# The first attention batch in a new order, held-back transposes and loads, and weight sums placed earlier

## The chip, the cores and the metric

The kernel runs on one core of a Trainium2 chip. The metric is the device time of one execution in microseconds (us). Nine executions of the kernel before took 974.5 to 976.42 us, with a median of 975.21. The engines are called as in the profile: PE is TensorE (PEld its weight load), DVE is VectorE, ACT is ScalarE, POOL is GpSimd, SP is SyncE. POOL and SP issue nearly all DMA transfers.

## The reference

Two parts follow each other. The first is a linear attention with cosine weights over 8 batches, 8 heads, 576 positions and a head width of 64; the second a mixture of 8 experts over the 4608 rows that come out, with gate weights that are balanced by eight rounds of Sinkhorn scaling.

```python
theta = np.pi / 2.0 * pos / S
phi(x) = concatenate([relu(x) * cos(theta), relu(x) * sin(theta)])   # q_p, k_p
kv  = einsum('bhsf,bhfd->...', k_p, v);  z = sum(k_p over s)
num = q_p @ kv;  den = q_p @ z + 1e-06;  x = num / den               # per batch and head
P = exp(x @ w_gate - max)
for _ in range(8): P /= P.sum(1) + 1e-09; P /= P.sum(0) + 1e-09; P *= N / E
out = sum over e of P[:, e] * (relu(x @ w1[e]) @ w2[e])
```

## The kernel before

**Attention and expert 0 are interleaved.** Batch 0 is computed alone. Then come blocks of 512 rows of expert 0, index j from 0. Each block has 16 slots: in slots 0 to 7 `ffn1` makes one eighth of the hidden layer (four products of 512 columns and a relu on ACT), in slots 8 to 15 `ffn2` makes half a tile of 128 output rows (four products; every second slot ends with a copy of the tile on ACT). A table, filled by `at(block, slot, ...)` in lines 641 to 788, hangs the attention work of batch j + 1 and the preparation of batch j + 2 behind the slots. Slots 0 to 3 of block 0 are done with batch 0's numerators (lines 677 to 695). The instructions of PE, DVE and ACT stand in the order in which the code writes them (`InOrder`, line 101). Those of POOL and SP are placed by the framework, which keeps their dependencies.

**Steps of one batch**, with the names of the profile. `load` (line 229) brings q, k and v in halves of two head pairs, six transfers a batch, issued by POOL; `held_back` lets a load wait for the latest DVE instruction written so far. Each of the names q_ld, k_ld and v_ld has four buffers. `prep_q` (line 377) makes q_p, the scaled q of one head pair, on DVE. For batches 0 and 1 PE turns it against an identity matrix (`turn`, line 420), and ACT or DVE copies the result out of a `small_ps` bank (there are four) with a relu. From batch 2 on SP turns it with a DMA transpose into q_pT (line 392). `prep_k` is the relu on k (ACT or DVE), `prep_kp` makes k_p on DVE, `prep_v` copies v beside a column of constants. `sums` makes the products of k_p and v for half the heads and copies them to kv_sb; for batch 0 the key sums z come from PE products of their own (`key_sums`). `denominators` (line 527) makes the products with z for all heads, then DVE's reciprocal den, and hi and hl, two parts of it. `spread_out` repeats hl over rows on PE, ACT copies it to rb; `numerators` multiplies q_pT by kv_sb on PE, and DVE multiplies by rb into xT, the input of the experts.

One line of the transposes ties them to a load:

```python
                if b == 3 and hk == 0:

                    after(landing["v", b, 1], turned)
```

With b counted from 0 this is the fourth batch and its first head pair. `after` is a real wait, `not_before` only an order on one engine.

**Fillers.** `keep_busy` (line 276) gives PE products of ones with ones whose result nobody reads, at the start and wherever batch 0 leaves PE without work.

**Experts 1 to 7** use sums of weight blocks and of row blocks, so that fewer products are needed. `w1_steps` and `w1_sums` build such sums of w1, `w2_first` replaces a block of w2 by a difference, and `Pair.step` builds three more sums of w2 (tiles V, lines 1004 to 1017) when the first pair of an expert arrives. `group` (line 916) makes the hidden layer of one quarter of the columns for 768 rows; it calls `fill()` seven times. While the first unit of expert 1 runs, `start_fill` (line 1188) deals out the last tiles of expert 0 in parts and the remaining steps of `sinkhorn` (line 1071). In a Sinkhorn round, `tw_steps` (line 1143) lists the weight sums done meanwhile: the first two of a round behind its column sums, the others behind its product on PE. After that unit, `w2_first` for expert 1 runs on DVE (line 1248).

Of the kernel before, what the change touches and what calls it, by code (L numbers as in the profile page):

```python
# [19 lines left out]
XS = 64.0  # L20
# [5 lines left out]
def kernel(  # L26
# [185 lines left out]
    with ExitStack() as p1:  # L212
        ld = p1.enter_context(tc.tile_pool(name="ld", bufs=4))
        kp_pool = p1.enter_context(tc.tile_pool(name="kp_pool", bufs=4))
        qp_pool = p1.enter_context(tc.tile_pool(name="qp_pool", bufs=3))
        qT_pool = p1.enter_context(tc.tile_pool(name="qT_pool", bufs=1))
        kv_pool = p1.enter_context(tc.tile_pool(name="kv_pool", bufs=2))
        rb_pool = p1.enter_context(tc.tile_pool(name="rb_pool", bufs=4))
# [7 lines left out]
        landing = {}  # L226
        sources = {"q": q, "k": k, "v": v}

        def load(b, half, names="qkv", held_back=False):
            for name in names:  # L230
# [6 lines left out]
                if held_back:  # L237

                    after(ve.last, i)
# [8 lines left out]
        load(0, 0, "q")  # L248
        gidx = cs_pool.tile([P, C], FP32, name="gidx")
# [4 lines left out]

        ones_sq = cs_pool.tile([P, P], F16, name="ones_sq")
# [6 lines left out]
        load(0, 1, "q")  # L262
        for name in "kv":
            load(0, 0, name)
            load(0, 1, name)
# [22 lines left out]
        for _ in range(74):  # L288
            keep_busy(1)
# [17 lines left out]
        for hh in range(2):  # L307
            ve.tensor_copy(
                out=cs_half[hh * HP : (hh + 1) * HP, :, :, hh],
                in_=cs[hh * HP : (hh + 1) * HP, :, :, 0],  # L310
            )
# [8 lines left out]
        C3 = C // 3  # L320

# [6 lines left out]
        with nc.allow_low_precision("sums of zeros and ones"):  # L328
# [11 lines left out]
        ones_col = const.tile([P, 1], FP32, name="ones_col")  # L340
        ve.memset(ones_col[:], 1.0)
        ones_all = const.tile([P, P], FP32, name="ones_all")
        ve.memset(ones_all[:], 1.0)
        eps_row = cs_pool.tile([1, 32], FP32, name="eps_row")
        ve.memset(eps_row[:], 1e-6 / XS)
# [8 lines left out]
        lent = acc_lo[:, G_LO - 4 : G_LO, :].rearrange("p g d -> p (g d)").bitcast(F16)  # L354
        VA = C * (D + 2)
        v_augs = [
            lent[:, i * VA : (i + 1) * VA].rearrange("p (c d) -> p c d", d=D + 2)
            for i in range(4)
        ]
# [7 lines left out]
        for t in v_augs:  # L367
            ve.memset(t[:, :, D : D + 1], 1.0 / XS)

# [7 lines left out]
        def prep_q(b, hk):  # L377
# [12 lines left out]
            if by_dma:  # L390
                qTs[b, hk] = q_pTs[(b * HK + hk) % len(q_pTs)]
                turned = nc.sync.dma_start(
                    out=qTs[b, hk], in_=q_p[:].rearrange("p c a d -> p (c a d)"),
                    transpose=True,
                )
                if b == 3 and hk == 0:

                    after(landing["v", b, 1], turned)
            else:
                qps[b, hk] = q_p  # L400
# [76 lines left out]
        def sums_begun(b, half):  # L477
# [7 lines left out]
            kv_ps = [ps_s.tile([P, 512], FP32, name="small_ps") for hh in range(2)]  # L485
# [157 lines left out]
        for hk in range(HK):  # L643
            if hk == 3:
                prep_k(0, 0)
                prep_k(0, 1)
                z_ps = key_sums(0)
                prep_q(0, hk)
                key_sums_made(0, z_ps)
            else:  # L650
                prep_q(0, hk)
            for i in range(3):
                turn(0, hk, i, True)
                keep_busy(3)
        prep_kp(0, 0)
        prep_kp(0, 1)
        denominators(0, range(0, 4))
        keep_busy(8)
        for hk in (2, 3):
            prep_k(0, hk)  # L660
        z_ps = key_sums(1)
        prep_kp(0, 2)
        key_sums_made(1, z_ps)
        prep_kp(0, 3)
        keep_busy(5)
        denominators(0, range(4, 8))
        for half in range(2):
            sums_made(0, half, sums_begun(0, half))
            keep_busy((0, 18)[half])
# [6 lines left out]
        ]  # L676
        for hk in range(HK):
            attend(0, hk)
            for kt in ((), (0,), (1,), (2, 3))[hk]:
                for ft, h_ps in enumerate(first_ps):  # L680
                    te.matmul(
                        out=h_ps[:],
                        lhsT=w0[0][:, kt, ft * P : (ft + 1) * P],
                        rhs=xT[:, kt, 0:TCH],
                        start=(kt == 0),
                        stop=(kt == KT - 1),
                    )
                    if kt == KT - 1:
                        se.activation(out=hT[:, ft, 0:TCH], in_=h_ps[:], func=AF.Relu)
            for i in ((), (0,), (1, 2), ())[hk]:  # L690
                prep_k(1, i, i < 2)
            for i in ((), (0,), (1,), (2, 3))[hk]:
                if i == 3:
                    prep_k(1, i, False)
                prep_kp(1, i)
# [3 lines left out]
        for j in range(B):  # L699
            b = j + 1  # L700
            if j == 0:
# [4 lines left out]
                for hk in range(HK):  # L706
                    for i in range(3):
                        at(0, (5, 6, 6, 7)[hk], turn, 1, hk, i, i != 1)
                    if hk == 0:
                        at(0, 5, prep_q, 1, 3)  # L710
                    if hk == 2:
                        at(0, 6, prep_v, 1, 0, se.copy)
                        at(0, 6, prep_v, 1, 2, ve.tensor_copy)
                    if hk == 3:
                        at(0, 7, prep_v, 1, 1, se.copy)
                        at(0, 7, prep_v, 1, 3, ve.tensor_copy)
# [6 lines left out]
            elif b < B:  # L723
# [14 lines left out]
                elif j == 2:  # L738
                    at(j, 0, sums, b, 1)
# [554 lines left out]
```

## Time and profile before

| | us |
|---|---|
| median of nine executions | 975.21 |
| lowest, highest | 974.5, 976.42 |
| the profiled execution, time | 974.5 |
| its span, first to last instruction | 972.8 |

The page gives each engine's busy time within the span. A line of the timeline reads: start in us, duration in us, engine, line, operation, written tile <- read tiles, shapes, count, and in brackets how long the engine had been idle and what released it. Many lines say L109, the helper through which every PE, DVE and ACT instruction is issued; there the tiles' names tell the step. The chain that ended last is mostly PE:

```profile
PE 91%; DMA 4%; issue 2%; DVE 1%; POOL 1%; ACT 0%; POOLq 0%; DVEq 0%; SPq 0%; ACTq 0%
```

The granted clock is 1.00 in all parts. The DMA queues are busiest in the first 45 us, when the loads of three batches and the weights of expert 0 arrive.

### The profile page before, as it was taken

What the parts mean: (1) busy time and instruction counts of PE and PEld (TensorE: products, weight loads), DVE (VectorE), ACT (ScalarE), POOL (GpSimd) and SP (SyncE); (2) the same over time, 40 slices, a digit from 0 to 9 for tenths busy, and PEclk for the clock granted to TensorE, in tenths of its full rate; (3) what the DMA queues carried; (4) which work ended last, traced back from release to release, by engine and by line L of the source; (5) the groups of instructions that cost most, each with busy time, mean ns of one, the idle gap of its engine ahead of it and who ended that gap; (6) DMA issues with size and microseconds to landing.
All of it is one profiled execution on the core that took longest, in us unless ns stands there. A gap on an engine that the chain in (4) does not pass through costs nothing.

```text
span 972.8 us, 20258 instructions
## 1 busy us (share of the span) xinstructions
PE 960.5 (99%) x7855; PEld 675.9 (69%) x7855; DVE 807.3 (83%) x1831; ACT 565.5 (58%) x1264; POOL 60.7 (6%) x82
## 2 busy tenths in 40 slices
PE   9999999999999999999999999999999999999997
PEld 6545545567777777777777777777777777777775
DVE  6777776789898987987888987987888987988887
ACT  5766665577776555555555555555555555555551
POOL 6231110010000000000000000000000000000001
PEclk9999999999999999999999999999999999999999
DMA  9999988231004301332004301322104401104435
GB/s 163 184 152 178 153 141 185 44 69 50 26 26 93 69 25 50 68 59 59 25 26 93 69 25 51 68 51 64 30 25 85 77 25 42 33 27 126 122 90 127
DMA packets 81200, 74.72 MB, mean 77 GB/s; under 512 B 33360, under 2 KB 73040, under 8 KB 81104
## 3 DMA queue, kind: packets, MB, share of 16 engines
q0 software_dynamic: 27232, 30.94, 20.4%
q1 hardware_dynamic: 53632, 42.24, 17.4%
q8 instruction: 61, 1.00, 0.4%
q14 instruction: 35, 0.29, 0.1%
q10 hardware_dynamic: 240, 0.26, 0.1%
HBM read 84.30 MB, written 12.98 MB: 100 GB/s over the span
## 4 chain that ended last, share of the span: by engine, by line
PE 91%; DMA 4%; issue 2%; DVE 1%; POOL 1%; ACT 0%; POOLq 0%; DVEq 0%; SPq 0%; ACTq 0%
PE rows_ps L109 34%; PE h_ps L109 28%; PE p_ps L109 11%; PE copied_ps L109 11%; PE y_ps L109 4%; PE small_ps L109 3%; DMA k_ld<-in_k_dram 1%; DMA w2e<-in_moe_w_dram 1%; DMA w1e<-in_moe_w_dram 1%; DVE acc_hi L975 0%; POOL q_ld L233 0%; POOL hs_last L990 0%; DMA out_dram<-acc_lo 0%; DVE H L905 0%; DVE S L203 0%
## 5 line engine op out<-in xcount | busy, mean ns | idle before, releaser
L975 DVE SCALAR_TENSOR_TENSOR acc_lo<-rows_ps,P_tok,acc_lo 128x512 f32<-128x512 f32 (+1 forms) x322 | 203.2, 639 | 75.0 <-PE rows_ps L109 74.9
L109 PEld LDWEIGHTS <-H 128*128 128x128 f16 x2080 | 203.2, 98 | 82.3 <-issue 1.4
L911 ACT CAST u<-h_ps 128x384 f16<-128x384 f32 x288 | 137.7, 478 | 129.6 <-PE h_ps L109 129.6
L109 PEld LDWEIGHTS <-w1e 128*128 128x128 f16 x1632 | 157.7, 98 | 67.3 <-issue 5.3
L905 DVE CUSTOM_DVE_ANT_0 H<-p_ps,u 128x384 f16<-128x384 f32 x329 | 180.9, 550 | 7.3 <-PE p_ps L109 7.2
L109 PEld LDWEIGHTS <-hs 128*128 128x128 f16 x1500 | 146.6, 98 | 56.2
L109 PE MATMUL p_ps<-xT,T 128*128 128x384 f16 x672 | 164.1, 326 | 1.0 <-DVE H L905 0.9
L109 PE MATMUL h_ps<-S,w1e 128*128 128x384 f16 x672 | 164.1, 326 | 0.8 <-ACT u L911 0.6
L109 PE MATMUL rows_ps<-V,H 128*128 128x256 f16 x1000 | 150.0, 273 | 0.7 <-DVE acc_hi L975 0.7
L109 PE MATMUL rows_ps<-w2e,hs 128*128 128x256 f16 x1000 | 150.0, 273 | 0.0
L109 PE MATMUL h_ps<-xT,w1e 128*128 128x384 f16 (+1 forms) x616 | 148.8, 350 | 0.1
L943 ACT ACTIVATE H<-h_ps 128x384 f16<-128x384 f32 x144 | 70.7, 491 | 94.5 <-PE h_ps L109 94.5
L109 PEld LDWEIGHTS <-T 128*128 128x128 f16 x1008 | 98.4, 98 | 31.8 <-issue 4.8
L109 PE MATMUL rows_ps<-w2e,H 128*128 128x256 f16 (+1 forms) x568 | 94.4, 285 | 0.0
L924 ACT COPY copied_ps<-h_ps 128x384 f32<-128x384 f32 x144 | 67.4, 468 | 35.9 <-PE h_ps L109 35.1
L934 ACT ACTIVATE H<-copied_ps 128x384 f16<-128x384 f32 x144 | 70.9, 492 | 20.3 <-PE copied_ps L109 20.3
L109 PE MATMUL h_ps<-S,T 128*128 128x384 f16 x336 | 81.8, 325 | 0.6 <-ACT copied_ps L109 0.5
L109 PE MATMUL copied_ps<-xT,w1e 128*128 128x384 f16 x336 | 82.1, 326 | 0.0
L109 PE MATMUL copied_ps<-w2e,H 128*128 128x256 f16 x504 | 75.5, 272 | 0.0
L109 PE MATMUL rows_ps<-V,hs 128*128 128x256 f16 x500 | 75.0, 272 | 0.0
L975 DVE SCALAR_TENSOR_TENSOR acc_lo<-copied_ps,P_tok,acc_lo 128x256 f32<-128x256 f32 x126 | 60.0, 476 | 0.4
L975 DVE SCALAR_TENSOR_TENSOR acc_hi<-rows_ps,P_tok,acc_hi 128x512 f32<-128x512 f32 (+1 forms) x56 | 41.3, 737 | 20.6 <-PE rows_ps L109 19.8
(146 smaller groups left out, 948.2 us busy)
## 6 DMA issues: line engine op xcount, KB each, us to landing
S<-x_saved SPq DMA_DIRECT2D x114, 192.0 KB, 2.3
out_dram<-acc_lo SPq DMA_DIRECT2D x62, 128.0 KB, 2.4
w1e<-in_moe_w_dram POOLq DMA_DIRECT2D x7, 1024.0 KB, 9.1
w2e<-in_moe_w_dram POOLq DMA_DIRECT2D x7, 1024.0 KB, 10.0
q_ld<-in_q_dram POOLq DMA_DIRECT2D x16, 288.0 KB, 6.6
k_ld<-in_k_dram POOLq DMA_DIRECT2D x16, 288.0 KB, 8.3
v_ld<-in_v_dram POOLq DMA_DIRECT2D x16, 288.0 KB, 9.3
x_saved<-S SPq DMA_DIRECT2D x12, 192.0 KB, 1.8
```

Of the source, the lines that this page charges most:

```text
L109: i = getattr(self.engine, name)(*args, **kwargs)
L905: latest = ve._custom_dve(TENSOR_ADD_SAT, out=out, in0=ps[:, 0:TU], in1=t[:], s0=FP32_MAX, s1=0.0)
L911: se.copy(out=t[:], in_=ps[:, 0:TU])
L924: se.copy(out=Y[:, 0:TU], in_=X[:, 0:TU])
L934: se.activation(out=h11, in_=Y[:, 0:TU], func=AF.Relu)
L943: se.activation(out=h12, in_=X[:, 0:TU], func=AF.Relu)
L975: ve.scalar_tensor_tensor(out=a, in0=rows, scalar=P_tok[:, g, self.e : self.e + 1], in1=a, op0=ALU.mult, op1=ALU.add,)
```

## The change

The change has these parts.

- **Buffers.** q_p gets four buffers instead of three, rb three instead of four.
- **Setup.** The second half of q is issued ahead of the position index, the first half of k ahead of the identity mask. The 74 fillers of 128 columns become 110 of 64. Memsets move up, and the copy into `cs_half` moves behind the second q_p (`halve`).
- **Batch 0.** The four q_p come first, k after them; the second half of `sums` moves behind the second spread and uses the `h_ps` banks; the first products of expert 0 start with the two `y_ps` banks. k_p of batch 1 moves behind them all.
- **Block 0.** PE's turns of batch 1 move from slots 5, 6, 6, 7 to 6, 6, 7, 7, and all four v copies go to DVE.
- **Blocks 1 to 6.** Block 2 gets the schedule of the later ones; the relus of k stand three to five slots later; the first half of the sums of the fourth batch moves from block 1 to block 2, and so do part of its k_p and v.
- **Transposes and loads.** From the fourth batch on every transpose waits for the fifth of its batch's six loads, and the loads of a later batch (from index 4 on) wait for the second transpose of the batch before instead of for DVE.
- **Expert 1.** `w2_first` and the three V sums of expert 1 move into the Sinkhorn rounds; the parts of expert 0's last tiles are dealt out at other fills.

```diff
-        qp_pool = p1.enter_context(tc.tile_pool(name="qp_pool", bufs=3))
+        qp_pool = p1.enter_context(tc.tile_pool(name="qp_pool", bufs=4))
...
-        rb_pool = p1.enter_context(tc.tile_pool(name="rb_pool", bufs=4))
+        rb_pool = p1.enter_context(tc.tile_pool(name="rb_pool", bufs=3))
...
-                if held_back:
+                if behind is not None:
+
+                    after(turnings[behind], i)
+                elif held_back:
...
-        for _ in range(74):
-            keep_busy(1)
+        for _ in range(110):
+            te.matmul(
+                out=idle_ps[:, 0:HP], lhsT=ones_sq[:],
+                rhs=ones_sq[:, 0:1].to_broadcast([P, HP]), start=True, stop=True,
+            )
...
-                if b == 3 and hk == 0:
-
-                    after(landing["v", b, 1], turned)
+                if b >= 3:
+
+                    after(landing["v", b, 0] if b < 5 else landing["k", b, 1], turned)
+                turnings[b, hk] = turned
...
         for hk in range(HK):
+            prep_q(0, hk)
+            if hk == 1:
+                halve()
             if hk == 3:
                 prep_k(0, 0)
                 prep_k(0, 1)
                 z_ps = key_sums(0)
-                prep_q(0, hk)
-                key_sums_made(0, z_ps)
-            else:
-                prep_q(0, hk)
             for i in range(3):
                 turn(0, hk, i, True)
-                keep_busy(3)
+                keep_busy(3 * (hk < 3))
         prep_kp(0, 0)
+        key_sums_made(0, z_ps)
+        for hk in (2, 3):
+            prep_k(0, hk)
         prep_kp(0, 1)
         denominators(0, range(0, 4))
-        keep_busy(8)
-        for hk in (2, 3):
-            prep_k(0, hk)
         z_ps = key_sums(1)
+        keep_busy(4)
+        key_sums_made(1, z_ps)
         prep_kp(0, 2)
-        key_sums_made(1, z_ps)
+        denominators(0, range(4, 8))
         prep_kp(0, 3)
-        keep_busy(5)
-        denominators(0, range(4, 8))
-        for half in range(2):
-            sums_made(0, half, sums_begun(0, half))
-            keep_busy((0, 18)[half])
+        sums_made(0, 0, sums_begun(0, 0))
+        keep_busy(20)
+        spread_out(0, 0)
+        numerators(0, 0)
+        keep_busy(4)
+        spread_out(0, 1)
+        sums_made(0, 1, sums_begun(0, 1, (ps_h[0], "h_ps")))
...
+        numerators(0, 1)
+        spread_out(0, 2)
+        first_l1(0, (2, 3, 0, 1))
+        numerators(0, 2)
+        spread_out(0, 3)
+        first_l1(1, range(4))
+        numerators(0, 3)
+        prep_k(1, 0)
+        prep_k(1, 1)
+        first_l1(2, range(4))
+        first_l1(3, range(4))
         for hk in range(HK):
...
+            if hk >= 2:
+                prep_k(1, hk, False)
+            prep_kp(1, hk)
         for hk in range(3):
             prep_q(1, hk)
...
-                        at(0, (5, 6, 6, 7)[hk], turn, 1, hk, i, i != 1)
+                        at(0, (6, 6, 7, 7)[hk], turn, 1, hk, i, i != 1)
                     if hk == 0:
-                        at(0, 5, prep_q, 1, 3)
...
+                        at(0, 6, prep_q, 1, 3)
+                    if hk in (1, 3):
+                        for i in (hk - 1, hk):
+                            at(0, (6, 7)[hk // 2], prep_v, 1, i, ve.tensor_copy)
...
-                at(j, 6 if j == 1 else 3 if j == 2 else 4, denominators, b)
+                at(j, 6 if j == 1 else 4, denominators, b)
...
+                    (4, prep_q, 0), (5, prep_q, 1), (9, prep_k, 0), (8, prep_q, 2),
+                    (10, prep_k, 1), (12, prep_q, 3), (12, prep_k, 2), (13, prep_k, 3),
+                    (13, prep_kv, 0), (14, prep_kv, 1),
                 ) if j == 1 else (
...
+                    (5, prep_q, 0), (6, prep_q, 1), (8, prep_k, 0), (8, prep_q, 2),
+                    (9, prep_k, 1), (10, prep_q, 3), (10, prep_k, 2), (11, prep_k, 3),
                     (11, prep_kv, 0), (14, prep_kv, 1),
...
-                if j == 1:
-                    at(j, 15, sums, b + 1, 0)
...
-                        at(j, 12, load, b + 2, half, name, True)
+                        at(j, 12, load, b + 2, half, name, True, (b + 1, 1))
             elif j and b + 2 < B:
                 for half in range(2):
-                    at(j, 11 + half, load, b + 2, half, "qkv", True)
+                    at(j, 11 + half, load, b + 2, half, "qkv", True, (b + 1, 1))
...
+    nothing = [lambda: None] * 2
+    tw_steps[2].append(lambda: w2_first(w_next))
+    tw_steps[4].append(lambda: w2_sums(w_next[1], 0))
+    tw_steps[5] = nothing + [lambda: w2_sums(w_next[1], 1)]
+    tw_steps[6] = nothing + [lambda: w2_sums(w_next[1], 2)]
...
-        for _ in range(1 + (k_fill % 14 == 1)):
+        for _ in range(1 + (k_fill in (1, 2, 23))):
...
-                w2_first(w)
```

`first_l1(kt, fts)` is the loop of the kernel before over the four banks for one kt, with the relu behind the last. `w2_sums(w2, part)` holds the DVE sums that stood in `Pair.step`: two for part 0 and 1 (V of lines 1007 and 1008), one for part 2 (line 1017); experts from 2 on still call them where they stood. `sums_begun` takes the banks as an argument.

## The prediction

> **What bounds the kernel now.** I read the busy times of the page first, then busy time by stretches of 10 us, then the timeline where PE (TensorE) is not full.
>
> ```profile
> PE 960.5 (99%) x7855; PEld 675.9 (69%) x7855; DVE 807.3 (83%) x1831; ACT 565.5 (58%) x1264; POOL 60.7 (6%) x82
> ...
> 50.00:60.00 10.00, 8.95 (x115) 4.46 (x114) 7.41 (x17) 5.12 (x13) 3.59 (x5) 1.00 1.05 144
> 60.00:70.00 10.00, 9.68 (x119) 4.86 (x119) 8.18 (x19) 7.66 (x20) 2.96 (x5) 1.00 0.99 167
> 180.00:190.00 10.00, 9.54 (x51) 4.87 (x50) 7.88 (x21) 6.74 (x13) 0.75 (x1) 1.00 0.40 65
> 200.00:210.00 10.00, 9.01 (x61) 5.65 (x59) 9.90 (x21) 6.09 (x15) 3.36 (x3) 1.00 0.79 145
> ```
>
> The columns of the stretches: PE, PEld, DVE, ACT, POOL busy, granted clock, DMA share, GB/s. PE has no work to lose in this change except fillers, so only its waits and the fillers can move the time. From 70 to 180 us its busy time reads 10.00 in every stretch: edits there gain nothing and can only harm. What can be won lies in four places: the start (fillers hide its waits), 58 to 62, 189, and 203 to 207. DVE is nearly full in the last.
>
> The start, in the timeline:
>
> ```profile
> 10.87 0.53 DVE L109 TENSOR_SCALAR k_ld<-k_ld 128x576 f16<-128x576 f16 x2 [1.63 <-DMA k_ld<-in_k_dram]
> 11.31 0.75 DVE L109 TENSOR_TENSOR q_p<-q_ld,acc_hi 128x1152 f16<-128x1152 f16 x1
> 15.41 0.75 DVE L109 TENSOR_TENSOR k_p<-k_ld,acc_hi 128x1152 f16<-128x1152 f16 x1
> 16.11 1.35 DVE L109 RECIPROCAL den<-y_ps 96x192 f32<-96x192 f32 x1
> 17.79 0.42 DVE L109 SCALAR_TENSOR_TENSOR hl<-hi,lo,den 96x192 f16<-96x192 f16 x1
> 33.47 1.03 PE L109 MATMUL small_ps<-acc_lo,k_p 64*128 64x65 f16 x54 [0.74 <-ACT acc_lo L109]
> 34.44 1.04 PE L109 MATMUL y_ps<-w2e,hT 128*128 128x512 f16 x4
> ```
>
> DVE waits for the first keys, then works without a break from 10.87 to 18.21, when hl, on which every later product hangs, is done. The fourth q_p and the fourth k_p stand in this row ahead of hl. The row at 34.44 is slot 8 of block 0, my mark for the end of the start.
>
> Near 58 us:
>
> ```profile
> 54.19 3.20 SPq L392 DMA_TRANSPOSE q_pT<-q_p  x1
> 58.61 0.68 ACT L109 ACTIVATE k_ld<-k_ld 128x576 f16<-128x576 f16 x1 [2.39 <-DMA k_ld<-in_k_dram]
> 59.66 0.70 ACT L109 COPY rb<-small_ps 128x384 f32<-128x384 f32 x2
> 60.20 0.46 PE L109 MATMUL small_ps<-hl,acc_hi 96*128 96x192 f16 x3 [1.25 <-ACT rb L109]
> ```
>
> ACT stands in order: the relu of the fourth batch's first keys (slot 8) waits for their load, the rb copy that PE needs (slot 9) stands behind it. Expert 1:
>
> ```profile
> 189.00 0.58 ACT L109 COPY acc_hi<-rows_ps 128x512 f32<-128x512 f32 x1
> 190.02 0.48 PE L109 MATMUL h_ps<-S,T 128*128 128x384 f16 x2 [0.48 <-ACT copied_ps L109]
> ...
> 201.40 0.72 DVE L109 TENSOR_TENSOR w2e<-w2e 128x1024 f16<-128x1024 f16 x1
> 203.58 0.68 DVE L1007 TENSOR_TENSOR V<-w2e 128x1024 f16<-128x1024 f16 x1
> 204.51 0.68 DVE L1008 TENSOR_TENSOR V<-V,w2e 128x1024 f16<-128x1024 f16 x1
> 206.38 0.48 PE L109 MATMUL p_ps<-xT,T 128*128 128x384 f16 x2 [0.85 <-DVE H L905]
> ```
>
> Three weight sums sit in DVE's queue ahead of the add that frees PE's bank; and a 0.58 us accumulator copy sits ahead of the copy PE waits for.
>
> **1. First batch.** Queue order of the loads is unchanged except that iota and the mask stand one load later; POOL's loads are held by the landing of earlier ones up to batch 2 (each issue follows the landing of the eighth load before it: 10.84 to 11.13, 12.30 to 12.58), so no landing moves. The keys still come at 10.84. The 110 fillers of 64 columns: the 128-column ones ran 106.7 ns apart up to 6.97 us and 57.7 ns after. Per filler, from below half of 106.7, so an end near 7.0; from above 96 ns (7.09 us over 74) if the weight load held the pace, an end at 11.7 and about 3 us lost. The nearest row for a full weight load with few columns is the gate product, 20 in 0.66 us (33 ns, doubled at the slow start): 88 of them until 6.97, 22 more in 0.7, end 7.7. I take that; it lies beside the wait for keys.
>
> With four q_p buffers and the new order, the fourth q_p (0.75) is done before 10.84. DVE after the landing: two relus 0.44, k_p 0.67, zsel 0.25 after the key sums on PE (0.73) to 12.4, two relus and k_p 1.1 to 13.6, second zsel after its key sums to 14.1, k_p 0.67, reciprocal, hi, hl 1.39 + 0.29 + 0.42: about 16.9, and the fourth k_p behind it. That is 1.3 earlier than 18.21. PE then has four spreads (0.35), four numerators (0.36), 16 products (0.22), and now the second half of the sums and a filler (0.8), which lay ahead of hl before: 7.2 us, to 24.2 against 25.6.
>
> Then the work put last comes due: the four k_p, two relus and three q_p of batch 1 all stand behind the last xT product (23.2), 5.1 us of DVE, to 28.35; before, k_p ran between the xT products. PE's slots 4 to 6 (2.7) end at 26.9, its turns need q_p (27.1, 27.7) and then a bank that DVE empties only at 28.9: a new wait of 0.7. Slot 7, the fourth q_p, four evictions and four v copies (DVE now has all four, 0.44 each) bring the second sums to 33.1 against 34.4: **-1.2**. Ends: -2.2 (the second quarter of w2 lands at 32.14) and +0.5 (DVE's queue gives all back).
>
> **2. Fourth batch.** Its loads start at 51.67 and land 1.40, 1.90, 1.57, 1.83 apart, those of batch 2 about 1.4 apart; the transpose at 54.19 ran beside them and took 10.3 us to land. Held back, the keys come no later than now, and their relu moves behind the rb copy of slot 9. The PE idle time of 50 to 70 is 1.05 + 0.32: **-1.4**. If the keys are 1 us late again, ACT has the copy of slot 10 behind them: 0 is the other end.
>
> **3. The new wait.** Behind a waiting transpose on SP stand only transposes; behind a load that waits for the second transpose, on POOL, only loads. Who waits for both: the denominators of batch 4 (index 3), in block 2 slot 4. Block 2 began at 67.8; less 1.2, less 1.4 and less the 0.7 of half a sums group that moves from block 1 into it: 64.5. Slot 4's denominators come 5.8 to 6.3 later (block 3: 86.38 to 92.19), so the last transpose must have landed at about 70.6. The fifth load lands near 60.3 (start 50.4, first landing 5.5 later, three more at 1.45); transposes issue 1.4 apart: 60.3, 61.7, 63.0, 64.4. The second lands near 65.0 and releases the loads of batch 5, which meet the fourth. What does a transpose beside loads cost? Without loads beside it 3.2 to 3.7. The Trainium skill (DMA: Bandwidth & Descriptors, section Queues, rings and completion order) says that each engine takes turns between its queues packet by packet; by that rule a shared transpose takes at most twice its own time, 6.6, lands by 71.0, costs up to 0.4, and holding it back is worth little. The trace disagrees for one issued amid loads (10.3), which would land at 74.7: 4.1 us lost. Nearest is the fourth transpose of this very batch: issued at 66.79, just ahead of loads from 67.04, landed 72.76: 6.0, hence 70.4. I take **+0.3**; ends 0 and 8 (it lands with the last of six loads, 78.6).
>
> Later batches: loads start about 1 us earlier than now; batch 5's last transpose would be issued near 81 and is needed near 89.6; slack over 2. Relus moved to slots 8 to 11 give ACT 2.8 + 2.1 (rb) + 1.2 (copies) within some 5 us, and slots 12 to 15 are free; k_p needs them later. A third rb buffer suffices, since two are alive between spread and numerators. **0**; ends 0 and +1.
>
> **4. Expert 1.** The first of fp32 tile copies ends in the sixth fill instead of the seventh, so it is ahead of the relu by a product; PE's 0.48 at 190.02 goes: **-0.5** (ends 0, -0.6). The weight sums (0.72 and three of 0.68) leave the DVE queue of 201 to 208. Idle there 0.99; with the slow product starts around them: **-1.3** (ends -0.4, -1.6). They now stand in the Sinkhorn steps near 174, 182, 187 and 192, in gaps of DVE such as 0.53 before 186.86 and 1.27 before 192.27; without that cover each is 0.7 on the product sharing its bank: **+0.1** (ends 0, +0.8).
>
> Sum: -1.2 - 1.4 + 0.3 - 0.5 - 1.3 + 0.1 = **-4.0 us** from the profiled execution's 974.5 (span 972.8 and 1.7 around it): 970.5. That execution is the lowest of the nine, 0.7 under their median; in terms of the median, **971.2**.
>
> **Rivals.** A, the start gives back everything: DVE's 5.1 us at 23.2 becomes the bound (+0.5 for -1.2). For it: three of its evictions are on PE's path; against: even with them slot 8 is early. 972.9. B, the batch-4 denominators wait for a transpose that lands with the loads of batch 5: +8 for +0.3 gives 978.9; slower than before from the point where it lands more than 4 us past 70.6. For it: the 10.3; against: the 6.0. C, a start bound only by w2's landing and no wait at the turns: -2.2 for -1.2, and no wait in step 3: 969.9. That the change does nothing would need both PE waits (1.25 and 0.85) to be replaced one for one; the chain shows no second late party there.
>
> **Numbers.** Forecast 0.47, A 0.20, B 0.16, C 0.12, other 0.05. A measurement of this kernel can tell 0.2% (2 us) from no change: faster is below 973.3, slower above 977.2. Forecast, C and two thirds of A are faster, with a little of the rest: 0.74; B's lower half and the rest of A: 0.14; slower 0.12. The range takes C with a little more gain, and A with half of B's small losses: 968.8 to 974.8.
>
> **What would show it.** Right: hl near 17 and slot 8 of block 0 near 33; no PE wait for rb near 57 to 60; denominators of block 2 without a gap; no wait of 0.85 for H near 203; 200 to 210 with PE above 9.7. Wrong: slot 8 at 34.4 or later with DVE full from 23; a PE gap ahead of block 2's denominators ended by a DMA; or a new gap between 182 and 195 behind DVE.

## The result and the profile after

The changed kernel takes 970.12 us (median of nine executions, 969.4 to 970.95); the kernel before took 975.48 beside it (29 executions). The ratio is 0.9943, with a 95% interval of 0.9934 to 0.9953: 5.4 us faster. The forecast was 971.2 in a range of 968.8 to 974.8. The profiled execution took 969.92 us, its span is 968.2 (before 974.5 and 972.8).

Busy times of the page, then busy time by stretches of 10 us, of the changed kernel, with the columns as in the prediction:

```profile
PE 958.2 (99%) x7886; PEld 674.2 (70%) x7886; DVE 808.9 (84%) x1834; ACT 565.1 (58%) x1261; POOL 60.4 (6%) x82
...
50.00:60.00 10.00, 10.00 (x121) 5.05 (x113) 7.22 (x16) 6.20 (x15) 3.32 (x5) 1.00 0.99 157
60.00:70.00 10.00, 9.98 (x137) 5.19 (x135) 7.51 (x18) 7.16 (x17) 4.31 (x6) 1.00 0.98 165
180.00:190.00 10.00, 10.00 (x59) 5.54 (x57) 8.45 (x19) 6.28 (x14) 0.76 (x1) 1.00 0.64 107
190.00:200.00 10.00, 9.59 (x55) 5.26 (x54) 8.54 (x20) 6.91 (x16) 4.06 (x3) 1.00 0.19 63
200.00:210.00 10.00, 9.94 (x73) 7.07 (x73) 8.67 (x20) 7.61 (x16) 0.00 (x0) 1.00 0.68 104
```

PE's idle time from 50 to 70 us is gone (1.37 before, 0.02 now). From 180 to 190 PE is full (9.54 before). In the rest of expert 1 some idle time is left: all work here stands four to five us earlier, so that the stage of 200 to 208 us before is now read at 195 to 203, and nearly all of the 0.41 us missing in the fourth stretch belongs to it.

The timeline of the changed kernel, the same operations that the prediction showed of before:

```profile
1.14 5.85 PE L109 MATMUL y_ps<-ones_sq 128*128 128x64 f16 x110 [1.14 <-DVE ones_sq L109]
...
10.31 0.53 DVE L109 TENSOR_SCALAR k_ld<-k_ld 128x576 f16<-128x576 f16 x2 [0.89 <-DMA k_ld<-in_k_dram]
...
15.74 0.41 DVE L109 SCALAR_TENSOR_TENSOR hl<-hi,lo,den 96x192 f16<-96x192 f16 x1
...
32.48 1.04 PE L109 MATMUL y_ps<-w2e,hT 128*128 128x512 f16 x4
...
55.88 0.71 ACT L109 COPY rb<-small_ps 128x384 f32<-128x384 f32 x2
56.47 0.71 ACT L109 ACTIVATE k_ld<-k_ld 128x576 f16<-128x576 f16 x1
56.85 0.41 PE L109 MATMUL small_ps<-hl,acc_hi 96*128 96x192 f16 x3
...
63.84 1.35 SPq L403 DMA_TRANSPOSE acc_hi<-q_p  x1
64.83 1.43 POOL L234 DMA_DIRECT2D q_ld<-in_q_dram  x2 [11.51 <-DMA q_pT<-q_p]
...
69.29 0.51 PE L109 MATMUL small_ps<-q_pT,zsel 128*32 128x192 f16 x12
```

hl is done 5.9 us after the keys land, where it took 7.4; slot 8 of block 0 begins at 32.48 instead of 34.44. On ACT the rb copy now stands ahead of the relu of the fourth batch's first keys, and PE's spread at 56.85 waits for nothing. The last three rows are those of the wait that the prediction feared: the fourth batch's last transpose, the loads that the second transpose released, and the denominators, which have no gap before them.

Where the time came from is read by comparing the starts of the same products in both traces:

| start of | before | after | lead | gained in the stage |
|---|---|---|---|---|
| slot 8 of block 0 | 34.44 | 32.48 | 1.96 | 1.96 |
| block 3 | 86.38 | 82.41 | 3.97 | 2.01 |
| first product of S and T (expert 1) | 185.46 | 181.35 | 4.11 | 0.14 |
| 97th product of S and w1e (expert 2) | 297.19 | 291.92 | 5.27 | 1.16 |
| end of the last product | 968.78 | 963.62 | 5.16 | -0.11 |
| end of the span | 972.8 | 968.2 | 4.6 | -0.6 |

The rest of this text uses these marks. The traced executions lie 4.6 us apart and the medians 5.4, since the traced execution of the kernel before is the fastest of its 29 (974.5 against 975.48): the table accounts for 4.6 us. A wait of PE that is given without a row is counted from start to start of its products, less the usual distance; the brackets of the rows read about 0.17 us less for the same wait, because a product's modelled end reaches into the gap. Block 2 alone can't be compared, since half a group of sums (0.7 us) moved into it; blocks 1 and 2 together can.

### The profile page after: what moved, and what is told of

Its sections match the earlier page's. It is cut to its first block, busy times and chain, and to the rows that moved or that the text cites. A ratio compares the mean times of both kernels' runs of the same rounds, so it can differ in the third digit from the quotient of the medians.

```text
span 968.2 us, 20321 instructions
## 1 busy us (share of the span) xinstructions
PE 958.2 (99%) x7886; PEld 674.2 (70%) x7886; DVE 808.9 (84%) x1834; ACT 565.1 (58%) x1261; POOL 60.4 (6%) x82
## 4 chain that ended last, share of the span: by engine, by line
PE 95%; DVE 2%; DMA 1%; ACT 1%; POOL 1%; issue 0%; POOLq 0%; ACTq 0%; SPq 0%; DVEq 0%
PE rows_ps L109 34%; PE h_ps L109 29%; PE p_ps L109 11%; PE copied_ps L109 11%; PE y_ps L109 5%; PE small_ps L109 4%; DMA k_ld<-in_k_dram 1%; ACT hT L109 0%; DVE acc_hi L987 0%; POOL hs_last L1002 0%; DMA out_dram<-acc_lo 0%; DVE acc_lo L987 0%; POOL q_ld L234 0%; DVE H L109 0%; ACT acc_lo L109 0%
## 5 line engine op out<-in xcount | busy, mean ns | idle before, releaser
L987 DVE SCALAR_TENSOR_TENSOR acc_hi<-rows_ps,P_tok,acc_hi 128x512 f32<-128x512 f32 (+1 forms) x56 | 41.3, 737 | 20.0 <-PE rows_ps L109 19.1
```

The source lines that it names most:

```text
L987: ve.scalar_tensor_tensor(out=a, in0=rows, scalar=P_tok[:, g, self.e : self.e + 1], in1=a, op0=ALU.mult, op1=ALU.add,)
```

## The experiments

Theory S is the forecast's account: each stall goes because the work ahead of it in one engine's queue was moved, and the held-back transposes are a small part. Theory H gives the gain of blocks 1 and 2 to the hold (transposes and loads that wait for each other).

**Transposes and loads bound as before, all else changed.**

```diff
-                if b >= 3:
-                    after(landing["v", b, 0] if b < 5 else landing["k", b, 1], turned)
+                if b == 3 and hk == 0:
+                    after(landing["v", b, 1], turned)
...
-                        at(j, 12, load, b + 2, half, name, True, (b + 1, 1))
+                        at(j, 12, load, b + 2, half, name, True)
...
-                    at(j, 11 + half, load, b + 2, half, "qkv", True, (b + 1, 1))
+                    at(j, 11 + half, load, b + 2, half, "qkv", True)
```

> The changed kernel, but with the transposes and loads bound as before: only the first transpose of the fourth batch waits, for its sixth load, and the loads wait for DVE instead of a transpose. Theory S (the schedule): the wait near 57 us is gone because the first keys' relu moved behind the rb copy of slot 9, so nothing comes back: block 2 starts within 0.3 us of 63.3 and the time stays within 0.5 us of 970.1. Rival H (the holding back): the wait is gone because the held-back transposes let the keys land earlier; without it the wait of 1.2 to 1.9 us returns ahead of block 2 and the time is 971.3 to 972.

Measured: 981.03 us, ratio 1.0066 [1.0048, 1.0085]: slower than the kernel before. Its timeline, PE rows and then a row of SP's queue (start, duration of the issue), and its stretches:

```profile
75.88 0.51 PE L109 MATMUL small_ps<-acc_lo,zsel 128*32 128x192 f16 x6 [6.18 <-DMA acc_lo<-q_p]
79.16 0.51 PE L109 MATMUL small_ps<-acc_hi,zsel 128*32 128x192 f16 x6 [2.77 <-DMA acc_hi<-q_p]
...
64.87 7.61 SPq L403 DMA_TRANSPOSE acc_hi<-q_p  x1
```

```profile
70.00:80.00 10.00, 1.34 (x13) 0.52 (x13) 0.29 (x1) 0.00 (x0) 0.00 (x0) 0.65 1.05 154
80.00:90.00 10.00, 10.00 (x67) 4.97 (x66) 7.96 (x17) 6.40 (x15) 0.00 (x0) 0.83 0.60 87
```

Up to block 2 it runs as the changed kernel does (block 2 begins at 63.23, there 63.33), so the stall at 58 goes without the hold, as S says. Then the denominators of batch index 3 wait 9 us for two transposes: issued at 63.06 and 64.87 while the loads of the next batch were issued (62.21 to 65.77), they landed at 75.84 and 79.12. With the idle time comes a lower granted clock, and block 3 begins 11.2 us later. This is the mechanism of rival B, but it comes where the hold is *missing*; neither theory had that.

**The hold alone, on the kernel before:**

```diff
-                if b == 3 and hk == 0:
-                    after(landing["v", b, 1], turned)
+                if b >= 3:
+                    after(landing["v", b, 0] if b < 5 else landing["k", b, 1], turned)
+                turnings[b, hk] = turned
...
-                        at(j, 12, load, b + 2, half, name, True)
+                        at(j, 12, load, b + 2, half, name, True, (b + 1, 1))
...
-                    at(j, 11 + half, load, b + 2, half, "qkv", True)
+                    at(j, 11 + half, load, b + 2, half, "qkv", True, (b + 1, 1))
```

> The kernel before with nothing but the new waits of transposes and loads. Theory S: the keys still land after ACT reaches their relu in slot 8, so most of the 1.25 us wait at 60 stays: 974.7 to 975.5 in terms of the median of before (975.5). Rival H: the wait is gone, about 973.8. If the denominators of the fourth batch, which still stand in slot 3 here, find the last transpose late, it is slower than before: up to 977.

Measured: 973.96 us, ratio 0.9982 [0.9972, 0.9991]. S missed here: the time is H's, and of the stall of 1.4 us at 58 only 0.6 is left. The fourth batch's keys land earlier (57.25 instead of 58.59), 0.5 of it because their loads start that much earlier. But PE then waits three times, 0.37 to 0.50 us, for k_p and the copies of v between 66 and 69. From slot 8 of block 0 to block 3 it takes 52.09 us, where it was 51.94 before: in the traces the hold alone gains nothing in blocks 1 and 2.

In the medians it does gain 1.2 us. Its 20 executions took 973.54 to 974.55 us, the 23 of the kernel before beside it 973.88 to 980.71, and the traced execution of that kernel, 974.5, is among its fastest. How much of the change's 5.4 us in the medians is the hold's is therefore open.

**The relus of k in block 1 at their old slots, all else changed:**

```diff
-  (4, prep_q, 0), (5, prep_q, 1), (9, prep_k, 0), (8, prep_q, 2),
-  (10, prep_k, 1), (12, prep_q, 3), (12, prep_k, 2), (13, prep_k, 3),
+  (4, prep_q, 0), (5, prep_q, 1), (8, prep_k, 0), (8, prep_q, 2),
+  (9, prep_k, 1), (10, prep_k, 2), (12, prep_q, 3), (12, prep_k, 3),
```

> The changed kernel with the four key relus of block 1 one slot earlier again (slots 8, 9, 10, 12 instead of 9, 10, 12, 13); transposes and loads held as in the change. Theory S: ACT stands at the first keys again (landing near 56.3, ACT there near 55.2), the rb copy and with it PE come 1 to 1.5 us late: block 2 starts near 64.6, 971.2 to 971.7. Rival H: keys land early enough, 970.1 and no PE wait above 0.4.

Measured: 971.55 us, ratio 0.9961 [0.9946, 0.9976]. The timeline of this kernel:

```profile
56.83 0.68 ACT L109 ACTIVATE k_ld<-k_ld 128x576 f16<-128x576 f16 x1 [2.88 <-DMA k_ld<-in_k_dram]
...
57.88 0.70 ACT L109 COPY rb<-small_ps 128x384 f32<-128x384 f32 x2
...
58.42 0.32 PE L109 MATMUL small_ps<-hl,acc_hi 96*128 96x192 f16 x2 [1.73 <-ACT rb L109]
```

The stall is back in the very form that the prediction read: the relu waits for its load, the rb copy behind it waits too, and so does PE. Blocks 1 and 2 take 41.09 us instead of 38.85, so without this move nothing of their gain is left (40.86 before). In block 1 the relus had moved by one or two slots only; three to five holds for the first two relus in the later blocks. These slots of ACT's queue are worth 2.2 us of the stage; in the medians the two kernels lie 1.4 us apart.

**Three q_p buffers in the changed kernel:**

```diff
-        qp_pool = p1.enter_context(tc.tile_pool(name="qp_pool", bufs=4))
+        qp_pool = p1.enter_context(tc.tile_pool(name="qp_pool", bufs=3))
```

> The changed kernel with three q_p buffers. As the prediction had it, the fourth buffer lets the fourth q_p be made before the keys land: with three it waits for PE's turn of the first, and if that is late hl ends up to 0.7 us after 16.2. Rival: the first buffer has been free since about 8.0 us, so the order alone did it: hl within 0.1 of 16.2 and the time as the changed kernel's, 970.

Measured once: 972.57 us. Two rows of its timeline:

```profile
63.46 0.76 DVE L109 TENSOR_TENSOR q_p<-q_ld,acc_hi 128x1152 f16<-128x1152 f16 x1 [1.56 <-DMA q_pT<-q_p]
...
69.12 0.46 PE L109 MATMUL small_ps<-acc_lo,k_p 64*128 64x65 f16 x18 [0.57 <-DVE acc_lo L109]
```

hl comes 5.88 us after the keys land (16.53 against 10.65), as with four buffers (5.87): batch 0 doesn't need the fourth. But the time is not that of the rival either. The loss lies in blocks 1 to 3 (60.29 us instead of 57.84). A held-back transpose keeps its q_p until it lands; with three buffers DVE waits at 63.46 for one, in the middle of the queue that makes k_p, the copies of v and zsel (the z that the denominators use), and PE waits for those. The fourth buffer is the price of the hold.

**The hold with its fourth buffer, on the kernel before** (the hold alone, and then):

```diff
-        qp_pool = p1.enter_context(tc.tile_pool(name="qp_pool", bufs=3))
+        qp_pool = p1.enter_context(tc.tile_pool(name="qp_pool", bufs=4))
-        rb_pool = p1.enter_context(tc.tile_pool(name="rb_pool", bufs=4))
+        rb_pool = p1.enter_context(tc.tile_pool(name="rb_pool", bufs=3))
```

> The kernel before with the held-back transposes and loads and, in addition, four q_p and three rb buffers; all else old. Theory F (the fourth q_p buffer belongs to the held-back transposes, which keep three buffers occupied): the waits of 0.37 to 0.50 us for k_p near 66 to 69 us, which the hold alone showed, go; block 3 begins at 84.5 to 85.2 instead of 86.03, and the time is about 972.5 to 973.2. Theory G (the fourth buffer is worth something to the first batch only, as the prediction had it): the waits stay, block 3 begins near 86, and the time is that of the hold alone, 974. Both: the first batch as before, hl some 7.2 us after the first keys land.

Measured: 973.48 us, ratio 0.998 [0.9971, 0.9989]. The waits at 66 to 69 are gone (F), but block 3 begins at 85.77, not near 85: block 1 takes 21.29 us (22.29 before), and the gain is given back at once in block 2 (19.63, before 18.57).

```profile
75.68 0.68 ACT L109 ACTIVATE k_ld<-k_ld 128x576 f16<-128x576 f16 x1 [1.65 <-DMA k_ld<-in_k_dram]
...
77.97 0.39 PE L109 MATMUL y_ps<-w2e,hT 128*128 128x512 f16 x1 [0.51 <-ACT hT L109]
```

It is the stall of slot 8 again, one block later: the loads of the next batch now start behind the second transpose, their keys land at 75.66 (9.5 us into block 2, where it was 8.4 in the kernel before), and a relu at its old slot holds up ACT and what PE needs from it (this time hT). So the hold needs the later relus in block 2 as well.

**One half of the hold at a time.** First the changed kernel with the loads bound as before and the transposes held:

```diff
-                        at(j, 12, load, b + 2, half, name, True, (b + 1, 1))
+                        at(j, 12, load, b + 2, half, name, True)
...
-                    at(j, 11 + half, load, b + 2, half, "qkv", True, (b + 1, 1))
+                    at(j, 11 + half, load, b + 2, half, "qkv", True)
```

> The changed kernel with its transposes held back until the fifth load, but with the loads of the next batch bound as in the kernel before, so that they start near 62.2 us. Theory T (a transpose issued among loads lands with the last of them; what saves the new schedule is that loads stay out until the transposes are issued): the third and fourth transpose, issued near 62.3 and 63.8, land at 74 to 79, the denominators of batch index 3 wait 6 to 9 us, and the time is 977 to 981. Theory U (it is the hold of the transposes, behind their own batch's loads, that saves them; the next loads hardly matter): they land by 70, no wait, time 970 to 971.

Measured: 980.54 us, ratio 1.0052 [1.0037, 1.0067]. Its timeline, rows of PE, of SP's and of POOL's queue:

```profile
76.46 0.51 PE L109 MATMUL small_ps<-acc_hi,zsel 128*32 128x192 f16 x6 [6.22 <-DMA acc_hi<-q_p]
...
63.38 1.66 SPq L403 DMA_TRANSPOSE acc_hi<-q_p  x1
...
62.59 1.43 POOL L234 DMA_DIRECT2D q_ld<-in_q_dram  x2 [9.72 <-DVE q_p L109]
```

The transposes issued at 59.02 and 60.44 landed 3.3 and 3.4 us later, the third, issued at 61.86 and 0.73 us ahead of the first load, 5.1 us later; the last one, issued 0.8 us after the first load, landed at 76.41, 13.0 us later. The loads landed from 68.68 to 78.31. Theory T holds for the last transpose, which alone makes the wait; the third it had wrong. U falls.

Then the loads behind the *fourth* transpose, and the transposes bound as before:

```diff
-                if b >= 3:
-                    after(landing["v", b, 0] if b < 5 else landing["k", b, 1], turned)
+                if b == 3 and hk == 0:
+                    after(landing["v", b, 1], turned)
...
-                    at(j, 11 + half, load, b + 2, half, "qkv", True, (b + 1, 1))
+                    at(j, 11 + half, load, b + 2, half, "qkv", True, (b + 1, 3))
```

> The changed kernel with its transposes bound as in the kernel before (only one waits, for the sixth load), but with the loads of the next batch behind the fourth transpose instead of the second. Theory T (loads must stay out until the transposes are issued, and nothing else is needed): the transposes issued from 61.7 to 65 us, with no load beside them, land by 68, the denominators of batch index 3 don't wait, block 2 takes 19.1 to 19.5 us, and the time is 970 to 971.5; the next batch's loads start near 65 to 67. Theory U (the hold of the transposes behind the fifth load is what matters): the wait of 6 to 9 us stays, time 977 to 981.

Measured: 976.79 us, ratio 1.0008 [0.9997, 1.002]: nothing of the gain is left, and neither theory's time. For the fourth batch T is right: three transposes issued from 61.98 to 64.88 with no load beside them landed 3.3 us later each, and the denominators don't wait. But then the roles change. The traced execution, 974.62, is the fastest of the ten, so 2.2 us of the median stay unread. The loads of the next batch start at 68.69 instead of 64.83, and a relu in block 2 waits 2.6 us for its keys; that batch's transposes, free to go, are issued at 74.14 and 77.48 among them and land at 85.14 and 86.14 (11.0 and 8.7 us later). The fourth lands at 88.59 and lets the loads after these start at 89.16 (81.89 in the changed kernel), too late for DVE:

```profile
98.74 0.31 DVE L109 TENSOR_SCALAR q_ld<-q_ld 128x576 f16<-128x576 f16 x1 [3.31 <-DMA q_ld<-in_q_dram]
...
100.37 0.51 PE L109 MATMUL small_ps<-hl,acc_hi 96*128 96x192 f16 x3 [2.48 <-DVE xT L109]
```

A relu on q waits for its load, the xT products behind it on DVE wait too, and PE for their banks. Blocks 2 and 3 take 20.5 and 22.4 us instead of 19.1 and 19.0. So T was too narrow: both halves are needed, transposes behind their own batch's loads and loads behind transposes.

**Batch 0 and block 0 in the old order, all else changed:**

```diff
-            prep_q(0, hk)
-            if hk == 1:
-                halve()
             if hk == 3:
                 prep_k(0, 0)
                 prep_k(0, 1)
                 z_ps = key_sums(0)
+                prep_q(0, hk)
+                key_sums_made(0, z_ps)
+            else:
+                prep_q(0, hk)
...
-                        at(0, (6, 6, 7, 7)[hk], turn, 1, hk, i, i != 1)
+                        at(0, (5, 6, 6, 7)[hk], turn, 1, hk, i, i != 1)
```

> The changed kernel with batch 0's order and block 0's slots as before; setup, fillers and everything from block 1 on as in the change. If the order is worth what is left after the landing, slot 8 of block 0 starts near 33.9 (32.48 with the new order, 34.44 in the kernel before): 1.2 to 1.5 us longer, 971.3 to 971.6. Rival: the earlier landing and the setup carry the start: below 33.0 and a time within 0.5 of 970.1.

**POOL's old order of the first loads, all else changed:**

```diff
         load(0, 0, "q")
-        load(0, 1, "q")
...
-        load(0, 0, "k")
...
-        load(0, 1, "k")
-        for half in range(2):
-            load(0, half, "v")
+        load(0, 1, "q")
+        for name in "kv":
+            load(0, 0, name)
+            load(0, 1, name)
```

> The changed kernel with the position index and the identity mask issued by POOL where they stood, ahead of the second q and the first k. If the earlier issue is why the keys landed at 10.29 instead of 10.84, they land near 10.8, hl ends near 16.7 and slot 8 of block 0 starts near 33.0 (32.48 in the changed kernel): 0.5 us longer. Rival: the landing comes from chance and the order of the setup is without effect: hl within 0.15 of 16.2.

Measured: 970.95 us for the first (ratio 0.9946 [0.993, 0.9963]), 970.12 for the second (once). These times alone say little, because the landing of the first keys differs between executions by as much as what is asked. In us from that landing:

| | keys land | to the end of hl | to slot 8 of block 0 |
|---|---|---|---|
| before | 10.84 | 7.36 | 23.60 |
| after | 10.29 | 5.87 | 22.19 |
| old order of batch 0 and block 0 | 10.65 | 7.15 | 23.97 |
| old order of the first loads | 10.35 | 5.87 | 22.21 |

The new order is worth 1.4 to 1.8 us. All fourteen kernels agree: slot 8 begins 22.2 to 22.7 us after the landing in the nine with the new order of batch 0, 23.3 to 24.0 in the five with the old one. Of the 1.96 us in the result table it makes 1.41; the other 0.55 is the earlier landing. In the ten kernels with the second q issued at 2.17 the keys landed at 9.58 to 10.65 (mean 10.04), in the four with it at about 2.62 at 10.34 to 10.84 (mean 10.54). The ranges overlap; whether the edit moves the landing stays open.

**The weight sums of expert 1 where they stood, all else changed:**

```diff
-    tw_steps[2].append(lambda: w2_first(w_next))
-    tw_steps[4].append(lambda: w2_sums(w_next[1], 0))
...
-                if self.first and self.e > 1:
+                if self.first:
...
+                w2_first(w)
```

> The changed kernel with expert 1's four weight sums of w2 where they stood (behind the first unit, on DVE ahead of the adds), the new fills kept. Of the 1.16 us that the two traces differ by between the first product with a weight sum and 292 us, the sums carry most: PE's wait for H near 202 returns (0.85 to 1.0), the two small waits of 192.7 and 199.4 go (0.7): 0.5 to 0.9 us slower, 970.6 to 971.0. Rival: the fills carry it, then this kernel is within 0.2 us of the changed one in the span up to 292.

**The old fills, all else changed:**

```diff
-        for _ in range(1 + (k_fill in (1, 2, 23))):
+        for _ in range(1 + (k_fill % 14 == 1)):
```

> The changed kernel with the parts of expert 0's last tiles dealt out at the old fills. The accumulator copy stands ahead of the copy PE waits for again: the wait of about 0.5 near 185 returns and the span up to the same product near 292 is 0.4 to 0.7 longer. Rival: with the weight sums in the rounds the bank is late anyway, then below 0.2.

**Both of these edits together, and batch 0 in its old order (the batch part of the diff further up) with block 0's new slots:**

> The changed kernel with the old order of batch 0 but the new slots of block 0, and with expert 1 as before (sums late, old fills). Two stages are read apart. Start: if the order inside batch 0 makes the whole gain, hl ends 7.2 us after the first keys land and slot 8 of block 0 begins 23.6 to 24.0 after them (22.2 in the changed kernel); if the new slots of block 0 carry a part, slot 8 begins near 22.8. Expert 1: from the first product of S and T to the 97th of S and w1e it was 111.73 us before and 110.57 after; with the sums alone late 111.13, with the fills alone old 110.61. If these two edits are all of it, this kernel shows 111.7; if something else in the change did part, 111.1 to 111.4. The time: 970.1 + 1.5 + 1.15 = 972.7.

Measured: 970.97 (ratio 0.9949 [0.9934, 0.9963]), 969.68 (once) and 972.03 (0.9967 [0.9955, 0.9979]). The start of the last one: hl 7.38 and slot 8 23.71 us after the keys' landing, so the order inside batch 0 carries most of that gain. Expert 1, from the first product of S and T to the 97th of S and w1e:

| | sums late | sums early |
|---|---|---|
| old fills | 111.45 (before: 111.73) | 110.61 |
| new fills | 111.13 | 110.57 (after) |

The sums are worth 0.84 us with the old fills and 0.56 with the new; the fills 0.32 and 0.04. The two gains overlap. The 0.28 between before and this rebuilt stage lies in the wait at the products of S and T that the prediction showed at 190.02: PE idle for 0.48 us before, 0.20 here. It comes with the buffers: the hold alone shows 111.72 for the stage, the hold with the fourth buffer 111.45. Why the buffers of the attention reach so far is open. With the sums late and the new fills, the wait that the prediction named is still there:

```profile
201.34 0.48 PE L109 MATMUL p_ps<-xT,T 128*128 128x384 f16 x2 [0.66 <-DVE H L917]
```

In the changed kernel it is gone. A product a little earlier waits for ACT instead, as in each of the two kernels with one edit undone (0.28 and 0.23; 0.09 in the kernel before):

```profile
200.03 0.48 PE L109 MATMUL h_ps<-S,w1e 128*128 128x384 f16 x2 [0.30 <-ACT u L109]
```

**Not tried:** the fillers of 128 columns in the new kernel. With 64 columns they end at 6.99 us, more than 3 us before the keys land, so they can't be on the path.

## Why the prediction was right, step by step

**1. First batch (forecast -1.2).** Right, also in its marks. The step had hl at 16.9 and slot 8 at 33.1 with the keys at 10.84; measured from the landing that is 6.1 and 22.3, and it was 5.9 and 22.2. Three statements in it were not right. The fillers ended at 6.99, not 7.7: they ran 53.3 ns apart, the lower bound, up to 6.57 us and 31 ns after; the gate product's 33 ns fits the last part, but its double, 66 ns, does not fit the slow one. It cost nothing. "With four q_p buffers": three do as well. And the "new wait of 0.7" at the turns (0.56 measured) stands at the same place in the kernel before; what went in its stead are two waits of 0.52 and 0.90 at the second sums, for what DVE and ACT copy. Whether "no landing moves" is right is open. Rival A, which gives the start back, falls: slot 8 kept the lead. Rival C (969.9) is nearer to the time than the forecast and is right that step 3 has no wait; its start is not: the wait at the turns is there, and the start gained 1.4 us from the landing, not 2.2.

**2. Fourth batch (forecast -1.4).** Mechanism right, as the relus at their old slots show; the term was too small. Blocks 1 and 2 gained 2.01 us. The sum took PE's idle time of the stretches (1.37). From start to start of the products the two stalls are longer: 1.63 and 0.37 us, where the same distances in the changed kernel are 0.21 and 0.17, so 1.62 together. The rest is spread over waits below 0.2 us.

**3. The new wait (forecast +0.3).** No wait came, for a reason that the step had half. By its own nearest row (70.4 against the 70.6 needed) there was none either; the +0.3 was a hedge. The release at 64.83 is where it said (65.0), but the last transpose landed at 67.14 instead of 70.4, and the denominators at 69.29 had 2.15 us to spare. The row that was called nearest, 6.0 us for one issued just ahead of loads, was too dear; behind the hold each took 3.3 to 3.5 us, the fourth too, although loads were issued 1 us after it. What differs is the head start. The fourth batch's transpose that was issued last ahead of the loads took 6.0 us with 0.3 us of head start (the kernel before), 5.0 and 5.1 with 0.6 and 0.7 (without the hold; with the loads free), and 3.2 to 3.3 with 0.9 to 1.0 in all ten kernels with the hold. The rule of the Trainium skill that was weighed there (DMA: Bandwidth & Descriptors, section Queues, rings and completion order: turns between the queues packet by packet) led to an estimate of at most 6.6 us, which holds for these and fails where loads come first: 12.8 and 14.3 us in the kernel without the hold, 13.0 with loads free. Whether the rule fails there or only the factor of two drawn from it, no run here shows. What follows from it, "holding it back is worth little", is wrong: without the hold the new schedule takes 981 us. "Stand only transposes" behind a waiting one was too narrow as well: DVE's next q_p waits for its buffer, as three buffers show. Later batches (forecast 0) gained 0.14 up to expert 1.

Rival B was priced at +8 and 978.9; its place and mechanism are real, and two kernels without the whole hold show them, at 981.0 and 980.5. That the changed kernel is free of it is the work of the hold, which the step took for a cost.

**4. Expert 1 (forecast -0.5, -1.3, +0.1: -1.7).** Measured -1.16. Both signs are right, the sum is mis-sized. Each term was too large by itself (0.32 for the fills, 0.84 for the sums), together they make 0.88 because they overlap, and the other 0.28 came with the buffers: the 0.48 us that the fills were to remove was down to 0.20 without them. What is late next (ACT's u, 0.30) was not looked for. The sums in the Sinkhorn rounds cost at most one small wait: the changed kernel has one of 0.07 us at 193.07, for DVE's H.

**The sum.** -4.0 was forecast; PE's last product came 5.16 earlier, of which 0.55 is a landing. The tail gave 0.6 back: the last store of the result landed 3.57 us after the last product, where it was 2.98 before. All kernels here show one of two tails, 4.0 to 4.1 or 4.6 us from the last product to the end. The short one belongs to the four kernels with the old slots of block 0, the long one to the ten with the new slots (the one with only batch 0 in its old order among them). Why is open.

That the traced times moved by 4.6 where 4.0 was forecast is in part luck: the landing and the tail, in no term, cancel, and blocks 1 and 2, 0.9 better than steps 2 and 3 said, cover expert 1, 0.5 worse than step 4 said.

## What to carry to other kernels

In a queue that runs in order, look at what stands between a late load and the copy that the busiest engine needs: moving a few relus by one or two slots was worth 2.2 us of the stage, and the hold with its buffer only moved the same stall to the next block. Keep DMA transposes and bulk loads apart in both directions, and count the buffers that held-back transposes keep. Two edits against neighbouring stalls need not add up: price the second against what is left.

## What the runs showed of the hardware

- **A transpose issued among loads waits for nearly all of them.** Issued with no load issued around it: 3.3 us to land, 2.0 of them after the issue (the three of the kernel with the loads behind the fourth transpose). Issued 0.9 to 1.0 us ahead of six loads: the same, in ten kernels; with a head start of 0.3 to 0.7 us: 5.0 to 6.0. Issued 0.8 us after the first of six loads: 13.0 us, with the loads landing up to 14.9 us after that point. In the kernel without the hold even its issue took 7.61 us in SP's queue.
- **Six to nine idle us of PE lower its clock.** In the kernel without the hold the granted clock reads 0.65 and 0.83 in the two stretches shown above, and products of 512 columns started 427 ns apart until 83.0 us, 216 from 83.4 on. So part of the 11.2 us is the slow restart. With the loads free (6.2 us idle) the clock reads 0.50 from 76.4 to 80.0 us; with the loads behind the fourth transpose (2.5 us idle) it stays at 1.00.
- **The first keys land anywhere between 9.58 and 10.84 us** in the kernels run here; a start that hangs on a load is compared from its landing.
